# A planned attention-and-MLP kernel: the planner's prices for ScalarE's exponentials and for PE's mode changes, and the issue order that follows from them

## The chip, the cores and the metric

The kernel runs on one core of a Trainium2 chip. A core has a matrix engine (PE, here with its weight loads shown apart as PEld), ScalarE (ACT), VectorE (DVE), GpSimd (POOL) and SyncE (SP), which issues most of the transfers. The engines run side by side, each through its own list of instructions in the order in which the program gives them, and wait for each other on semaphores. The metric is the device time of one execution in microseconds (us), as the median of several runs; before the change it was 745.36 us over 3 runs (745.0 to 745.64). A profile of one execution shows every instruction with its start and its duration. Its span is the time from the first instruction's start to the last one's end.

## The reference

Two branches see the same x (2048 tokens of 512 values, bfloat16) and are mixed by a gate. Branch A is attention with 32 heads of 16 values. Branch B is a normalised MLP with a shift between tokens, and then a second MLP with 1792 hidden values.

```python
x = A_x
g = sigmoid((x * gate_w).sum(-1, keepdims=True))
# A: 32 heads of 16
scores = einsum("bhqd,bhkd->bhqk", q, k) * 16 ** -0.5
o = einsum("bhqk,bhkd->bhqd", softmax(scores), v)
a = o.reshape(B, S, D) @ wo
# B: h = gelu(layernorm(x) @ w1), its quarters shifted by 1, -1, 2, -2 tokens
x1 = x + hs @ w2
b = x1 + gelu(layernorm(x1) @ w3) @ w4
out = g * a + (1 - g) * b
```

## The kernel before

*Tiles.* Attention is cut into 32 rounds: four chunks of 512 queries (c), four groups of eight heads (G), and the even or the odd heads of a group (p). A round has four heads (i = 0 to 3, each on 32 of PE's rows) by 16 blocks of 128 keys (kt): 64 tiles of 128 keys by 512 queries, 2048 in all. For each tile PE multiplies k by q into one of the eight PSUM banks (line 1372). Then the exponential is taken, and PE multiplies the result by V into the round's accumulator (line 1596).

*Two ways to an exponential.* `issue_act` gives two tiles at once (or three) to ScalarE, as one instruction (line 1467); each of its tiles goes through V once. `issue_dve` gives one tile to VectorE, which writes a first approximation of the exponential as the bits of a bfloat16 number (line 1498, called p1). `close_pair` then makes three shifted copies for two such tiles together, on VectorE (line 1541) or on GpSimd (line 1543). All four versions go through V and are summed there, so such a tile costs four multiplications by V. Which tiles go which way is not fixed: it comes out of the planner.

*The planner.* When the program is built, `Sim` plays all engines against each other with a price for each job and writes down the order in which they started; that order is each engine's list of instructions. A job's `hold` is the time after which its engine takes the next job, `lat` what passes from there until others may read the result. `try_engine` starts an engine's best job, sets `t_free` and tells when the job's banks come free: for ScalarE 100 ns behind its hold (`EARLY`), and for a matmul that writes into the bank 195 ns behind it (`USABLE`). `pe_run` plays PE. The four 32-row or 32-column quarters of the array work side by side, 216 ns for a matmul of 512 columns, and a change between q·k (mode "row") and the rest (mode "col") costs `SWITCH`. `pe_pick` decides what PE does next: q·k for ScalarE when banks are free, then q·k for VectorE, and otherwise multiplications by V (`do_pv`) and matmuls of the projections and the MLPs (`do_gen`), as many passes as fit into the time until the next exponential ends (`tr`). An exponential's hold is one line:

```python
hold = 0.833 * 512 * w + 51.5
```

*Knobs.* Some 40 numbers steer these choices. They start from `BASE`, and `STEPS` changes some of them at each of 256 stages of 8 tiles. Those that are spoken of here: `DVE_ALONE` (q·k for VectorE alone may be issued when VectorE comes free in less than so many ns), `DVE_WAIT` (how many tiles may stand waiting for p1), `GP2` (the share of pairs with two of the three shifts on GpSimd; otherwise one), `CAP3` (banks that ScalarE may hold so that three tiles are given at once; 0 means never).

*Around it.* The accumulator of a round goes out through VectorE (line 1617), a division with four small transfers, and a product on GpSimd (line 1635). The rest of ScalarE's list is a few copies at the start, five Gelus over the MLPs' hidden values (line 1214) with their table loads, and two outputs at the end (line 1992).

Of the kernel before, what the change touches and what calls it, by code (L numbers as in the profile page):

```python
# [98 lines left out]
class Job:  # L99
    __slots__ = ("eng", "hold", "lat", "deps", "prio", "fn", "acq", "frees", "at", "done", "start", "seq", "ready", "name", "port", "watch", "deps_tiles", "size", "need", "know")  # L100

    def __init__(self, eng, hold, lat, deps, fn, prio=5, acq=(), frees=(), at=0, name="", port=False):
        self.port = port
        self.eng, self.hold, self.lat, self.deps, self.fn = eng, hold, lat, list(deps), fn
        self.prio, self.acq, self.frees, self.at = prio, list(acq), list(frees), at
        self.done = self.start = None
        self.seq = 0
        self.ready = None
        self.name = name
        self.watch = []  # L110
        self.size = 0
        self.need = None
        self.know = 0

# [75 lines left out]
class Sim:  # L190
    SWITCH = {"row": 104.0, "col": 104.0, "full": 96.0}
    ISSUE = 4.0
    EARLY = {"ACT": 100.0, "DVE": 75.0}
    USABLE = {"ACT": 195.0, "DVE": 168.0}

    def __init__(self, slots):
# [5 lines left out]
        self.t_free = {e: 0.0 for e in ("ACT", "DVE", "POOL", "SP", "PE")}  # L202
        self.t = 0.0
# [126 lines left out]
    def try_engine(self, e):  # L330
# [33 lines left out]
        self.t_free[e] = self.t + j.hold  # L364
        if j.port:
            self.lock = self.t + j.hold
            if e == "DVE":
                self.dve_lock = self.t + j.hold + j.lat
        self.busy[e] += j.hold
        self.log.append((e, self.t, j.hold, j.name))  # L370
        self.push(self.t + j.hold, None)
        soon = [b for b in j.frees if isinstance(b, Call) or b.cls == "bank"] if e in self.EARLY else []
        if soon:
            for b in soon:
                if isinstance(b, Buf):
                    self.bank_know[b.slot] = max(self.bank_know[b.slot], j.know)
                    self.usable[b.slot] = max(self.usable[b.slot], self.t + j.hold + self.USABLE[e])
# [3 lines left out]
        end = self.t + j.hold + j.lat  # L381
# [71 lines left out]
def kernel(  # L453
# [80 lines left out]
        3: dict(SL0=0, B_LOW=3, DVE_WAIT=3, AHEAD=16, MAXU=9, ACC2=0),  # L534
        4: dict(P1_PRIO=0.136),
        5: dict(E_PRIO=0.1),
        6: dict(MAXU=3),
        7: dict(GP2=1, B_LOW=5),
        8: dict(E_PRIO=0.25, JOIN=1),
        9: dict(GP2=0.655),  # L540
        10: dict(GP2=1),
        11: dict(DVE_ALONE=-158),
        12: dict(LIMD=4),
        13: dict(AFIRST=0),
        14: dict(AFIRST=1),
        16: dict(DVE_STOP_L=16, PV_IDLE=0.117, PRESS=26),
        17: dict(IDLE_NS=864, B_LOW=8, ROT=0),
        18: dict(S_PRIO=0.38),
        19: dict(GP3=0.9),
        21: dict(GP3=0.8),  # L550
        22: dict(URG_L=18, PRESS=18),
        24: dict(GP3=0.9, URG_L=12, PRESS=26),
        25: dict(GP3=0.8, DVE_STOP=13, URG_L=18, PRESS=18),
        26: dict(AHEAD2=24, DUE_SH=32, GATE=3),
        27: dict(ROT=1),
        28: dict(SL0=-75, LIMA=2),
        29: dict(MAXG=2),
        30: dict(GP3=0.9, DUE_SH=-9),
        31: dict(GP3=0.8, DUE_SH=32),
        32: dict(GP3=0.967),  # L560
        33: dict(GP3=0.9, DUE_SH=-9),
        34: dict(PV_FULL=0.86, DUE_SH=16),
        35: dict(DVE_ALONE=2, ROT=0),
        36: dict(IDLE_NS=537, ROT=2, GATE=2),
        37: dict(P1_PRIO=0.55, ROWM=3),
        38: dict(SL1=-75, PV_FULL=0.813),
        39: dict(GP3=1, MAXG=1),
        40: dict(ROT=1),
        41: dict(S_PRIO=0.625, SL0=0, B_LOW=3, HOLE=2),
        42: dict(P1_PRIO=0.743, S_PRIO=0.3, GP3=0.8, DVE_STOP=4, DVE_STOP_L=14, URG=8, URG_L=12, DVE_ALONE=362, SL0=-75,  # L570
            IDLE_NS=374, AHEAD=12, PV_FULL=0.97, PV_IDLE=0.731, HOLE=3, MAXG=2, E_PRIO=2, AFIRST=2, ROWM=99, LIMA=4,
            JOIN=0),
        43: dict(ROT=2, AGE=6000),
        44: dict(MAXU=2, AGE=3000),
        45: dict(DVE_STOP_L=16, CAP2=5),
        46: dict(DVE_STOP_L=14, MAXU=3, CAP2=6, AGE=6000),
        47: dict(DVE_STOP=13, IDLE_NS=459, LIMA=3),
        48: dict(E_PRIO=0.4),
        49: dict(AT_SH=118),
        50: dict(ROT=3, ACC2=1),  # L580
        51: dict(GP3=1),
        52: dict(DVE_ALONE=-158, GATE=3, AGE=3000),
        53: dict(PV_FULL=0.813),
        54: dict(P1_PRIO=0.312, AHEAD=24),
        55: dict(BRES=2, MAXG=1),
        56: dict(URG=3, URG_L=18, SL1=-150, ROT=0),
        57: dict(URG_L=12, SL1=60, AGE=20000),
        58: dict(ROT=1),
        59: dict(SL1=130, B_LOW=2, PV_FULL=0.947),
        61: dict(LIMA=2),  # L590
# [24 lines left out]
        88: dict(AHEAD=9),
        89: dict(MAXU=9),
        90: dict(AGE=6000),
        91: dict(LIMA=2),
        93: dict(ROT=2),
        94: dict(ROT=0),  # L620
        95: dict(URG=2),
        96: dict(MAXU=2, JOIN=1),
        97: dict(MAXU=9, JOIN=0),
        98: dict(P1_PRIO=0.55, DVE_WAIT=4, PV_FULL=0.86),
        99: dict(LIMA=4),
        100: dict(URG=8, AT_SH=118),
        101: dict(P1_PRIO=0.414, AT_SH=0, ACC2=0),
        102: dict(AFIRST=1),
        103: dict(P1_PRIO=0.55, B_LOW=0, AHEAD=16, AT_SH=118, AFIRST=2, ACC2=1),
        104: dict(B_LOW=8, AHEAD=9),  # L630
        105: dict(E_PRIO=0.4),
        106: dict(JOIN=1),
        109: dict(CAP2=4),
        110: dict(GP3=0.9),
        111: dict(DVE_ALONE=362, SL1=60),
        112: dict(E_PRIO=2),
        113: dict(DVE_ALONE=500, SL1=-75, PRESS=11),
        114: dict(PV_IDLE=0.117, LIMD=3),
        115: dict(GP3=0.967, DUE_SH=-6),
        116: dict(LIMA=2),  # L640
        117: dict(GP3=0.9, DUE_SH=32, AFIRST=0),
        118: dict(GP3=0.8, B_LOW=5),
        119: dict(URG_L=18, IDLE_NS=700),
        120: dict(DVE_ALONE=2, SL0=-75, BRES=4, AGE=12000),
        121: dict(MAXU=7, ROWM=7, ACC2=0),
        123: dict(GP2=0, DUE_SH=16),
        124: dict(GP2=0.315),
        125: dict(GP2=1, DUE_SH=32, ROWM=5),
        126: dict(GP2=0.5),
        127: dict(DUE_SH=-9),  # L650
        128: dict(GP3=0.9, DVE_STOP_L=12, AT_SH=34),
        129: dict(GP3=0.8, DVE_STOP_L=14, AT_SH=118),
        130: dict(S_PRIO=0.214, GP2=1, GP3=0.9, URG=11, DVE_ALONE=-158, EARLY=64, SL0=0, SL1=0, IDLE_NS=374, BRES=0,
            DVE_WAIT=3, AHEAD=16, PV_FULL=0.97, PV_IDLE=0.5, PRESS=18, MAXU=3, CAP2=6, LIMD=4, GATE=3, ACC2=1, LIMA=3,
            JOIN=0),
# [1370 lines left out]
```

## Time and profile before

| what | value |
|---|---|
| median of 3 runs | 745.36 us |
| span of the profiled execution | 742.9 us |
| TensorE's granted clock | 1.00 in all stretches |
| transfers | 34.60 MB, 47 GB/s on the mean |

The page gives no time of the profiled execution apart from its span. The 2.5 us between span and median are taken as the time that lies around the span.

A line of a group reads: line of the kernel, engine, operation, tile written and tiles read, shape, number; behind the first bar the busy time in us and the mean duration of one in ns; behind the second the time in us that the engine stood idle just before them, and whose end finished the idle time. Busy time counts overlapping instructions once, so it can be far below number times duration. A line of the timeline reads: start and length of a stretch in us, engine, line, operation, number.

### The profile page before, as it was taken

How to read it: one execution, taken by the hardware profiler on the slowest of the kernel's cores; microseconds unless marked ns; L12 is line 12 of the kernel's file. 1: busy time of each engine (PE TensorE's matmuls, PEld its weight loads, DVE VectorE, ACT ScalarE, POOL GpSimd, SP SyncE). 2: the span in 40 equal slices, each digit the busy share in tenths (PEclk: the TensorE clock that was granted, in tenths of full speed). 3: DMA queues.
4: the chain of work that ended last, by engine and by line, in shares of the span. 5: the costliest groups of instructions: out<-in, count | busy, mean ns of one | idle time of the engine just before them, and what ended most of it. 6: DMA issues, size and time to landing. Idle time of an engine off the chain costs nothing.

```text
span 742.9 us, 23801 instructions
## 1 busy us (share of the span) xinstructions
PE 732.1 (99%) x9550; PEld 212.8 (29%) x9550; DVE 678.8 (91%) x1407; ACT 729.8 (98%) x767; POOL 479.0 (64%) x478
## 2 busy tenths in 40 slices
PE   9999999999999999999999999999999999999997
PEld 5443232232222222222322222222222232222222
DVE  5899999999999999898998988999999997999995
ACT  7999999999999999999999999999999999999996
POOL 2247657788776757678557776667777767564441
PEclk9999999999999999999999999999999999999999
DMA  9520234022102132124100110002100000011001
GB/s 199 157 58 5 67 85 91 20 48 67 56 20 63 42 78 55 50 80 95 31 18 14 30 46 15 26 22 48 24 24 18 22 20 20 21 28 24 22 11 43
DMA packets 67094, 34.60 MB, mean 47 GB/s; under 512 B 46748, under 2 KB 62380, under 8 KB 66984
## 3 DMA queue, kind: packets, MB, share of 16 engines
q1 hardware_dynamic: 66040, 32.56, 17.6%
q8 instruction: 74, 1.21, 0.7%
q10 hardware_dynamic: 944, 0.52, 0.2%
q14 instruction: 36, 0.29, 0.1%
HBM read 17.40 MB, written 6.81 MB: 33 GB/s over the span
## 4 chain that ended last, share of the span: by engine, by line
PE 82%; ACT 13%; DVE 3%; issue 2%; ACTq 0%; DVEq 0%
PE banks L1596 29%; PE banks L1372 28%; PE banks L1002 24%; ACT prob L1467 10%; ACT hB L1214 2%; DVE prob L1541 1%; DVE prob L1498 1%; PE banks L981 0%; PE banks L1033 0%; ACT L1214 0%; ACT hT L1214 0%; ACT L1216 0%; PE banks L1127 0%; DVE accsb L1973 0%; DVE accsb L1976 0%
## 5 line engine op out<-in xcount | busy, mean ns | idle before, releaser
L1467 ACT ACTIVATE prob<-banks 128x1024 bf16<-128x1024 f32 (+1 forms) x744 | 685.3, 1146 | 1.1 <-PE banks L1002 0.8
L1543 POOL TENSOR_SCALAR prob<-prob 128x1024 uint16<-128x1024 uint16 x416 | 426.9, 1048 | 218.8 <-DVE prob L1541 97.0
L1498 DVE TENSOR_SCALAR prob<-banks 128x512 uint16<-128x512 f32 x553 | 367.1, 684 | 37.1 <-PE banks L1372 31.9
L1596 PE MATMUL banks<-prob,V 128*17 128x512 bf16 (+1 forms) x3713 | 313.5, 381 | 0.3
L1372 PE MATMUL banks<-q,kT 32*128 32x512 bf16 x2048 | 277.8, 384 | 3.6 <-ACT prob L1467 1.6
L1541 DVE TENSOR_SCALAR prob<-prob 128x1024 uint16<-128x1024 uint16 x418 | 158.4, 431 | 2.9 <-PE banks L1596 0.9
L1372 PEld LDWEIGHTS <-kT 32*128 32x128 bf16 x2048 | 69.9, 91 | 305.6 <-ACT prob L1467 282.0
L1596 PEld LDWEIGHTS <-V 128*17 128x17 bf16 (+1 forms) x3713 | 70.3, 88 | 116.3 <-issue 97.1
L1002 PE MATMUL banks<-xnT,w 128*32 128x512 bf16 x1152 | 96.5, 383 | 0.0
L1002 PE MATMUL banks<-w,hT 128*32 128x512 bf16 x692 | 59.7, 383 | 0.0
L1002 PEld LDWEIGHTS <-w 128*32 128x32 bf16 x1936 | 42.6, 95 | 50.3 <-issue 29.3
L1635 POOL TENSOR_TENSOR oT<-accsb,bcs 128x512 bf16<-128x512 f32 x31 | 39.5, 1275 | 26.1 <-DVE prob L1541 15.8
L1002 PE MATMUL banks<-w,w 128*32 128x256 bf16 (+1 forms) x784 | 41.0, 308 | 0.5 <-DVE prob L1498 0.4
L1002 PE MATMUL banks<-w,hB 128*32 128x512 bf16 x448 | 36.2, 382 | 0.4 <-ACT hB L1214 0.4
L1013 PE MATMUL banks<-wo,oD 32*128 32x512 bf16 x64 | 24.2, 384 | 0.0
L1617 DVE COPY accsb<-banks 128x512 f32<-128x512 f32 x31 | 21.2, 683 | 1.9 <-PE banks L1596 1.4
L1174 DVE BATCH_NORM_STATS2 st<-x_sb 128x6 f32<-128x512 bf16 x32 | 21.4, 678 | 0.0
L1002 PEld LDWEIGHTS <-hT 128*32 128x32 bf16 x692 | 14.7, 95 | 20.5 <-issue 14.2
L1268 DVE CAST hB<-banks 128x512 bf16<-128x512 f32 x28 | 18.9, 682 | 1.0 <-PE banks L1002 0.9
L1268 DVE CAST hT<-banks 128x512 bf16<-128x512 f32 x28 | 19.1, 682 | 0.7 <-PE banks L1002 0.5
L1002 PE MATMUL banks<-wo,oD 128*32 128x512 bf16 x176 | 19.5, 383 | 0.0
L1214 ACT ACTIVATE hT<-hT 128x7168 bf16<-128x7168 bf16 (+1 forms) x3 | 19.4, 6454 | 0.0
(94 smaller groups left out, 258.9 us busy)
## 6 DMA issues: line engine op xcount, KB each, us to landing
bcs<-rr SPq DMA_DIRECT2D x124, 64.0 KB, 2.0
xn_dram<-xn SPq DMA_DIRECT2D x32, 128.0 KB, 1.9
w<-in_B_w_dram SPq DMA_DIRECT2D x5, 512.0 KB
oD<-oT SPq DMA_DIRECT2D x124, 16.0 KB, 1.8
w<-in_B_w_dram SPq DMA_DIRECT2D x4, 448.0 KB
out_dram<-ot SPq DMA_DIRECT2D x14, 128.0 KB, 1.7
x_sb<-in_A_x_dram SPq DMA_DIRECT2D x3, 512.0 KB
w<-in_A_wqkv_dram SPq DMA_DIRECT2D x2, 256.0 KB
```

What stands on the lines that cost most here:

```text
L1002: units.append([Op("col", j, lambda j=j, lf=lf, rf=rf, n0=n0, n1=n1, st=st, sp=sp: nc.tensor.matmul(get()[32 * j:32 * j + 32, n0:n1], lhsT ...
L1013: o = Op("row", i, lambda: nc.tensor.matmul(get(), lhsT=lf(0, P)[rows], rhs=rf()[rows], start=False, stop=True, tile_position=(32 * i, 0), ...
L1174: a = dve(600, deps, lambda: nc.vector.bn_stats(out=sb.slot[:], in_=x_sb[:, t, :]), prio=6, at=at, acq=[sb])
L1214: g = nc.scalar.activation(out=ap, in_=ap, func=ACT.Gelu_apprx_tanh)
L1268: pre.append(evac(g, PSUM_NS, lambda ps, m=m: nc.vector.tensor_copy(out=h2()[:, m, :], in_=ps[:])))
L1372: o = Op("row", i, lambda: nc.tensor.matmul(dst(), lhsT=kT[G][32 * i:32 * i + 32, kt * P:(kt + 1) * P], rhs=qbuf[G, c].slot[32 * i:32 * i ...
L1467: job = act(hold, ops, lambda: nc.scalar.activation(out=prob[:, pb.cut(), :].bitcast(BF16), in_=unit()[:, rb.cut(), :], func=ACT.Exp, scal ...
L1498: return nc.vector.tensor_scalar(out=prob[:, b0.cut() if w == 2 else b0.bufs[h0].slot, :], in0=unit()[:, rb.cut() if w == 2 else rb.bufs[0 ...
L1541: return nc.vector.tensor_scalar(out=cut(k), in0=cut(0), scalar1=float(SHIFT * k), scalar2=None, op0=ALU.add)
L1543: return nc.gpsimd.tensor_scalar(out=cut(k), in0=cut(0 if both else 2), scalar1=1.0, scalar2=float(SHIFT * (k if both else 1)), op0=ALU.mu ...
L1596: return nc.tensor.matmul(one(accs[r])[32 * i:32 * i + n, :], lhsT=lhs(n), rhs=rhs(), start=st and not edge, stop=True, tile_position=(0, ...
L1635: n = gp(1250, d3, lambda: nc.gpsimd.tensor_tensor(out=ob.slot[:], in0=ab.slot[:], in1=bb.slot[:], op=ALU.mult), acq=[ob], frees=[ab, bb], ...
```

## The change

The planner gets another model of ScalarE's exponentials and other prices for PE's changes of mode; with these a new set of `STEPS` is written in. What a job is and what it computes stay as they are.

```diff
 class Sim:
-    SWITCH = {"row": 104.0, "col": 104.0, "full": 96.0}
+    SWITCH = {"row": 95.0, "col": 96.0, "full": 96.0}
     ISSUE = 4.0
+    EXP = SimpleNamespace(step=63.5, begin=50.5, least=171.0, back=369.0, bank=56.0, early=39.0, prob=54.0)
     EARLY = {"ACT": 100.0, "DVE": 75.0}
     USABLE = {"ACT": 195.0, "DVE": 168.0}
...
-        self.t_free[e] = self.t + j.hold
...
+        if j.cols:
+            px, x = j.cols / 1.2, self.EXP
+            last = max(self.act_end + px + x.step, self.t + px + x.least)
+            self.act_end = last
+            self.t_free[e] = max(self.t + px + x.begin, last - x.back)
+            usable, early, end = last + x.bank, last - x.early, last + x.prob
+            self.busy[e] += px + x.step
+        else:
+            self.t_free[e] = self.t + j.hold
...
+            if e == "ACT":
+                self.act_end = self.t + j.hold + 60.0
+            if e in self.EARLY:
+                usable, early = self.t + j.hold + self.USABLE[e], self.t + j.hold + self.EARLY[e]
+            end = self.t + j.hold + j.lat
+        j.over = end
...
-            self.push(self.t + j.hold + self.EARLY[e], lambda: self.release(soon))
+            self.push(early, lambda: self.release(soon))
...
     STEPS = {
-        0: dict(S_PRIO=0.3, DVE_STOP_L=7, SL0=0, IDLE_NS=374, AHEAD=16, AT_SH=69, AFIRST=1, AGE=20000),
-        1: dict(SL0=45, B_LOW=5, DVE_WAIT=1, AHEAD=9),
-        2: dict(AHEAD=7, MAXU=4, ACC2=1),
...
+        0: dict(S_PRIO=0.3, GP2=1, DVE_STOP_L=7, SL0=0, IDLE_NS=864, BRES=2, AHEAD=16, AT_SH=69, HOLE=3, CAP3=5,
+            AFIRST=1, AGE=20000),
+        1: dict(DVE_STOP=2, URG=3, GATE=3, E_PRIO=0.1),
+        2: dict(MAXU=4),
...
+        job.cols = 512 * w
...
-        tr = min((j.start + j.hold + j.lat for j in exps if j.start is not None and j.done is None), default=None)
+        tr = min((j.over for j in exps if j.start is not None and j.done is None), default=None)
```

An exponential of two tiles (1024 columns, `px` = 853.3 ns) now ends 916.8 ns after the one before it, or 1024.3 ns after its own start, whichever is later. ScalarE may take the next job 369 ns before that end, its banks are told free 39 ns before it and may be written 56 ns after it, and its result may be read 54 ns after it. `tr`, the time until which PE's other passes must fit, goes by this end too. `STEPS` has 678 entries before and 1726 after. The knobs named above, as means over the 256 stages:

| knob | before | after |
|---|---|---|
| `DVE_ALONE` (ns) | -37 | 88 |
| `DVE_WAIT` | 3.13 | 3.20 |
| `GP2` | 0.82 | 0.61 |
| stages with `CAP3` of 3 or more | 8 | 35 |

More of the change, by code (lines that the diff above doesn't have):

```diff
@@ L99 @@
 class Job:
-    __slots__ = ("eng", "hold", "lat", "deps", "prio", "fn", "acq", "frees", "at", "done", "start", "seq", "ready", "name", "port", "watch", "deps_tiles", "size", "need", "know")
+    __slots__ = ("eng", "hold", "lat", "deps", "prio", "fn", "acq", "frees", "at", "done", "start", "seq", "ready", "name", "port", "watch", "deps_tiles", "size", "need", "know", "cols", "over")
     def __init__(self, eng, hold, lat, deps, fn, prio=5, acq=(), frees=(), at=0, name="", port=False):
@@ L113, in __init__ @@
         self.know = 0
+        self.cols = 0
+        self.over = None
 class Op:
@@ L376, in try_engine @@
                     self.bank_know[b.slot] = max(self.bank_know[b.slot], j.know)
[L377 removed]
+                    self.usable[b.slot] = max(self.usable[b.slot], usable)
             j.frees = [b for b in j.frees if b not in soon]
[L379 removed]
+            self.push(early, lambda: self.release(soon))
         self.pending -= 1
[L381 removed]
         if e == "SP" and j.hold > 1.5:
@@ L542 @@
[L542 to L554, printed above, removed]
@@ L642 @@
[L642 to L655, printed above, removed]
@@ new lines @@
+        8: dict(P1_PRIO=0.136, GP2=1, DVE_STOP=6, URG=2, DVE_ALONE=-81, SL0=0, B_LOW=5, AHEAD2=16, PRESS=18, MAXU=7,
+            ROT=2, GATE=2, E_PRIO=0.25, AFIRST=1, ROWM=99, LIMA=3, JOIN=1),
+        9: dict(AGE=12000),
+        10: dict(SL0=45),
+        11: dict(GP2=0.655, DVE_STOP_L=12, URG_L=18, DVE_ALONE=2, EARLY=64, SL0=0, BRES=4, AHEAD2=24, MAXU=3, ROT=1,
+            AT_SH=0, AGE=20000),
+        12: dict(PRESS=22, MAXU=5, CAP2=4),
+        13: dict(P1_PRIO=0.279, GP2=0.8, DVE_WAIT=4, ROWM=3),
@@ new lines @@
+        15: dict(P1_PRIO=0.743, S_PRIO=0.178, GP2=0.655, GP3=0.9, DVE_STOP=8, DVE_STOP_L=16, URG=3, URG_L=12, SL0=-150,
+            B_LOW=0, BRES=0, DVE_WAIT=1, AHEAD=3, PRESS=18, MAXU=3, ROT=0, CAP2=6, LIMD=4, ROWM=99),
+        16: dict(SL1=-75, AHEAD=7, MAXU=7),
+        17: dict(P1_PRIO=0.136, DVE_STOP=6, DVE_STOP_L=12, URG=2, DVE_ALONE=-158, SL0=0, SL1=60, IDLE_NS=864,
+            DVE_WAIT=3, AHEAD=16, MAXU=3, ROT=1, HOLE=2),
+        18: dict(DVE_STOP=8, E_PRIO=0.1),
+        19: dict(SL0=130, AHEAD2=32, AFIRST=0),
@@ new lines @@
+        37: dict(MAXG=3, AFIRST=0, LIMA=2, JOIN=1),
+        38: dict(BRES=4, PRESS=22, AFIRST=1),
+        39: dict(P1_PRIO=0.55, GP2=0.655, GP3=1, URG=5, SL1=-75, IDLE_NS=700, B_LOW=5, BRES=0, DVE_WAIT=2,
+            PV_FULL=0.947, PRESS=18, MAXG=1, E_PRIO=0.25, AGE=20000, ROWM=3, LIMA=3),
+        40: dict(GP2=1, GP3=0.967, DVE_STOP=8, URG=8, URG_L=12, DVE_ALONE=138, IDLE_NS=537, B_LOW=8, DVE_WAIT=3,
+            AHEAD=12, PV_FULL=0.813, PV_IDLE=0.25, AT_SH=118, HOLE=0, AFIRST=2, LIMA=2, JOIN=0),
@@ new lines @@
+        70: dict(AGE=3000, ROWM=5),
+        71: dict(P1_PRIO=0.414, DVE_STOP=6, URG=8, DVE_ALONE=-158, SL0=45, SL1=45, IDLE_NS=700, DVE_WAIT=3,
+            PV_FULL=0.947, PV_IDLE=0.25, MAXU=2, ROT=1, DUE_SH=16, HOLE=7, GATE=2, E_PRIO=0.4, AGE=20000, ROWM=99,
+            ACC2=1, LIMA=2),
+        73: dict(ACC2=2),
+        74: dict(EARLY=64, B_LOW=1, E_PRIO=2),
+        75: dict(P1_PRIO=0.1, URG_L=18),
+        76: dict(CAP2=6, ACC2=0),
+        77: dict(AGE=12000),
+        78: dict(GP3=0.633, AHEAD2=32, HOLE=3),
@@ new lines @@
+        79: dict(SL1=0, JOIN=1),
+        80: dict(GP3=1, ACC2=1),
+        81: dict(SL0=0),
+        82: dict(P1_PRIO=0.279, GP3=0.967, DVE_STOP=8, URG_L=12, EARLY=99, B_LOW=8, DVE_WAIT=2, AHEAD=24, AHEAD2=24,
+            PV_IDLE=0.117, MAXU=3, DUE_SH=32, CAP2=4, AGE=20000, ROWM=3, LIMA=4, JOIN=0),
+        83: dict(DVE_WAIT=4, CAP2=6),
+        84: dict(DUE_SH=-14),
+        85: dict(PRESS=15),
+        86: dict(S_PRIO=0.625, GP2=0.15, GATE=3),
+        87: dict(P1_PRIO=0.136, S_PRIO=0.38, GP2=1, GP3=1, DVE_ALONE=-81, IDLE_NS=537, AHEAD=3, PV_IDLE=0.5, PRESS=26,
+            ROT=0, DUE_SH=-9, AT_SH=0, HOLE=7, GATE=2, AGE=6000, ROWM=99, ACC2=2, LIMA=3),
@@ new lines @@
+        95: dict(S_PRIO=0.625, GP3=1, DVE_ALONE=2, EARLY=64, SL1=0, BRES=4, DVE_WAIT=3, AHEAD2=32, PV_IDLE=0.25,
+            PRESS=18, ROT=0, DUE_SH=32, AGE=3000),
+        96: dict(DVE_STOP_L=12, URG=2, AHEAD=12, MAXG=3, AFIRST=0, AGE=9000, JOIN=2),
+        97: dict(SL0=60, DVE_WAIT=1),
+        98: dict(P1_PRIO=0.55, S_PRIO=0.38, GP2=0.655, DVE_STOP_L=7, DVE_ALONE=-158, EARLY=99, BRES=0, DVE_WAIT=4,
+            AHEAD=9, AHEAD2=24, PV_FULL=0.86, PV_IDLE=0.5, MAXU=3, MAXG=1, AFIRST=2, AGE=6000, JOIN=0),
@@ new lines @@
+        99: dict(DVE_STOP_L=14, AT_SH=0, E_PRIO=0.4),
+        100: dict(S_PRIO=0.5, AGE=12000, LIMA=4),
+        101: dict(P1_PRIO=0.2, GP3=0.5, JOIN=2),
+        102: dict(P1_PRIO=0.55, S_PRIO=0.178, GP2=0.15, GP3=1, DVE_STOP_L=12, URG=8, SL0=0, PV_FULL=0.813, MAXU=9,
+            AT_SH=34, MAXG=2, E_PRIO=2, AGE=6000, JOIN=0),
+        103: dict(URG_L=18, DVE_ALONE=500, ACC2=0),
+        104: dict(S_PRIO=0.3, URG_L=12, SL0=-150, SL1=-150),
+        105: dict(SL0=-75, DVE_WAIT=2, AHEAD2=16),
+        106: dict(PRESS=15, LIMA=2),
@@ new lines @@
+        119: dict(GP2=0.3, GP3=0.8, URG=2, DVE_ALONE=362, IDLE_NS=700, B_LOW=5, DVE_WAIT=2, AHEAD=9, AHEAD2=24,
+            PRESS=11, ROT=0, AGE=20000, LIMA=2),
+        120: dict(GP2=1, DVE_ALONE=2, DVE_WAIT=4, AHEAD2=13, PV_FULL=0.947, PRESS=26, CAP2=6, CAP3=4, ROWM=3, ACC2=2),
+        121: dict(HOLE=2, LIMA=3),
+        122: dict(GP2=0.3, SL0=-150, ROWM=5),
+        123: dict(S_PRIO=0.5, GP3=1, DVE_STOP=4, URG=8, URG_L=18, SL0=0, B_LOW=8, AHEAD2=24, PV_FULL=0.86, PRESS=11,
+            MAXU=2, AT_SH=69, HOLE=3, CAP2=5, CAP3=0, GATE=4, ROWM=7, ACC2=1, LIMA=2),
@@ new lines @@
+        124: dict(GP2=0, URG=2, URG_L=12, MAXU=3, GATE=2, JOIN=2),
+        125: dict(PRESS=18, DUE_SH=-14, AGE=9000, JOIN=1),
+        127: dict(DVE_WAIT=3, E_PRIO=0.25, AFIRST=1, ACC2=2, LIMA=3, JOIN=2),
+        128: dict(DVE_STOP=8, DVE_STOP_L=16, SL0=-75, DVE_WAIT=4, PRESS=15, DUE_SH=16, AFIRST=0, AGE=20000, ACC2=1,
+            LIMA=2, JOIN=1),
+        129: dict(URG_L=18, SL0=0, PV_IDLE=0.25, PRESS=18, CAP3=4),
+        130: dict(DVE_STOP_L=14, AHEAD=16, ACC2=0),
+        131: dict(MAXU=2, CAP2=4),
@@ new lines @@
+        146: dict(SL1=-75, PV_IDLE=0.117, MAXU=2, RES=0, AGE=12000),
+        147: dict(DVE_ALONE=-81, B_LOW=2, JOIN=1),
+        148: dict(S_PRIO=0.38),
+        149: dict(S_PRIO=0.178, DVE_STOP_L=12, DVE_ALONE=500, SL1=130, IDLE_NS=864, B_LOW=8, AHEAD=24, MAXU=3, AGE=6000,
+            JOIN=2),
+        150: dict(CAP2=5, E_PRIO=0.25, ACC2=2),
+        151: dict(DVE_STOP=6, SL1=-75),
+        152: dict(CAP3=4, LIMD=5, E_PRIO=2),
+        153: dict(AHEAD=3, DUE_SH=32),
+        155: dict(S_PRIO=0.3, SL0=60, ROWM=7),
@@ new lines @@
+        156: dict(P1_PRIO=0.414, S_PRIO=0.178, GP3=1, DVE_STOP=2, DVE_STOP_L=7, URG=3, URG_L=12, SL0=0, SL1=130,
+            B_LOW=0, BRES=2, DVE_WAIT=2, AHEAD=24, ROT=1, DUE_SH=-14, AT_SH=0, HOLE=3, MAXG=1, CAP3=0, LIMD=3, ROWM=3,
+            ACC2=0, LIMA=4),
+        157: dict(URG_L=18),
+        158: dict(URG=8, DUE_SH=16),
+        160: dict(LIMD=4),
+        161: dict(S_PRIO=0.38, GP2=0.8, GP3=0.9, DVE_STOP_L=12, URG=11, URG_L=12, DVE_ALONE=362, EARLY=64, SL1=45,
+            IDLE_NS=537, BRES=0, PV_FULL=0.813, PV_IDLE=0.5, PRESS=18, MAXU=7, ROT=3, DUE_SH=-9, AT_SH=118, CAP2=6,
+            LIMD=3, AGE=3000, ROWM=7, ACC2=1, LIMA=2, JOIN=0),
@@ new lines @@
+        162: dict(GP2=0.3, BRES=2, MAXU=9),
+        163: dict(MAXU=7, CAP2=5, CAP3=4, LIMD=4),
+        164: dict(SL0=60, MAXU=2),
+        165: dict(MAXU=5),
+        166: dict(P1_PRIO=0.743, DVE_ALONE=2, SL0=0, DUE_SH=0, AT_SH=69, AFIRST=1, LIMA=3),
+        167: dict(P1_PRIO=0.414, GP2=0.655, DVE_STOP=4, DVE_STOP_L=7, URG=2, DVE_ALONE=362, SL0=45, SL1=-75, BRES=0,
+            AHEAD=7, AHEAD2=13, PV_FULL=0.916, PV_IDLE=0.117, PRESS=22, MAXU=7, DUE_SH=-9, AT_SH=118, CAP2=6, CAP3=0,
+            LIMD=5, E_PRIO=0.4, ACC2=0, LIMA=2, JOIN=2),
@@ new lines @@
+        168: dict(DVE_STOP_L=14),
+        169: dict(SL1=60, B_LOW=2, AHEAD=16, ROWM=99),
+        170: dict(S_PRIO=0.178, SL0=60),
+        171: dict(GP2=0.8, AGE=12000, ACC2=2),
+        172: dict(S_PRIO=0.38, DVE_STOP_L=12, URG=5, DVE_ALONE=2, EARLY=99, SL0=0, SL1=-75, B_LOW=0, DVE_WAIT=4,
+            AHEAD=24, AHEAD2=16, PV_FULL=0.813, PV_IDLE=0.25, PRESS=18, MAXU=3, ROT=1, AT_SH=34, HOLE=7, CAP2=4, LIMD=3,
+            E_PRIO=2, AFIRST=0, AGE=3000, ROWM=7, ACC2=1, JOIN=0),
+        173: dict(GP3=0.633),
@@ new lines @@
+        174: dict(GP3=0.9, DVE_ALONE=-81),
+        175: dict(SL0=60),
+        176: dict(GP3=0.967, DVE_ALONE=138, SL0=0, DVE_WAIT=3, PV_FULL=1, PV_IDLE=0.5, DUE_SH=16, CAP2=6, E_PRIO=0.4,
+            ACC2=0, LIMA=4, JOIN=2),
+        177: dict(GP3=0.9, URG_L=18, PV_FULL=0.813),
+        178: dict(EARLY=64, PV_FULL=0.97, LIMD=4),
+        179: dict(GP2=0, GP3=1, URG=3, URG_L=12, DVE_ALONE=500, PV_FULL=1, PRESS=26, MAXU=7, ROT=2, MAXG=3, CAP2=4,
+            LIMD=5, ACC2=1, LIMA=2),
+        180: dict(GP2=1, DVE_ALONE=2, EARLY=99, SL1=45, AHEAD=9, AHEAD2=32, MAXU=3, ROT=0, MAXG=1, CAP2=6, CAP3=5,
+            ACC2=2, LIMA=4),
```

435 lines of the change are left out of this document (219 added, 216 removed).

## The prediction, made before the changed kernel was run

> **What bounds the kernel now.** I read the page's busy shares first, then its chain of waits, then ScalarE alone, since the change is about ScalarE's exponentials.
>
> ```profile
> span 742.9 us, 23801 instructions
> PE 732.1 (99%) x9550; PEld 212.8 (29%) x9550; DVE 678.8 (91%) x1407; ACT 729.8 (98%) x767; POOL 479.0 (64%) x478
> PE 82%; ACT 13%; DVE 3%; issue 2%; ACTq 0%; DVEq 0%
> ```
>
> Three engines stand above 90%, so shares alone name no culprit, and the chain gives most to PE because it follows the last thing that each instruction waited for. The groups of ScalarE by form (busy time, mean duration in ns, then idle time ahead of the group and who ended it) say more:
>
> ```profile
> L1467 ACT ACTIVATE prob<-banks 128x1024 bf16<-128x1024 f32 x739 | 679.8, 1143 | 1.1 <-PE banks L1002 0.8
> L1214 ACT ACTIVATE hB<-hB 128x7168 bf16<-128x7168 bf16 x2 | 12.4, 6177 | 0.0
> L1467 ACT ACTIVATE prob<-banks 128x1536 bf16<-128x1536 f32 x5 | 8.0, 1593 | 0.0
> ...
> L1214 ACT ACT_TABLE_LOAD x3 | 3.8, 1283 | 0.1
> ...
> L1045 ACT COPY w<-banks 128x512 bf16<-128x512 bf16 x2 | 1.2, 586 | 2.2 <-PE banks L1033 2.2
> L1992 ACT ACTIVATE ot<-banks,omg 128x512 bf16<-128x512 f32 x1 | 0.7, 688 | 3.7 <-PE banks L1989 3.7
> L1467 ACT ACTIVATE prob<-banks x744: 1003/1144/1657, 8.7 to 733.6; 128x1024 bf16<-128x1024 f32 x184, 128x1536 bf16<-128x1536 f32 x2
> 459.45 7.55 ACT L1467 ACTIVATE prob<-banks 128x1024 bf16<-128x1024 f32 x8
> ```
>
> From the first exponential (8.7 us) to the last (733.6) ScalarE stood idle only 1.1 us ahead of any of the 744; the 13.1 us that it lacks to the span lie almost wholly before and after. And the 1143 ns of one are no price: 679.8 / 739 is 0.920 us, because they overlap. The last row shows it directly, eight in a row in 7.55 us with a last one of 1.14, that is (7.55 - 1.14) / 7 = 0.916 from end to end. So the pipe of exponentials is full all the time. Its tiles number 739 x 2 + 5 x 3 = 1493, and together they hold the engine 685.3 us:
>
> ```profile
> L1467 ACT ACTIVATE prob<-banks 128x1024 bf16<-128x1024 f32 (+1 forms) x744 | 685.3, 1146 | 1.1 <-PE banks L1002 0.8
> ```
>
> which is 0.459 us a tile. The span reads 742.9 = 685.3 of exponentials + 44.5 of other ScalarE work (729.8 - 685.3: Gelus, table loads, copies) + 13.1 idle. **No order of the same exponentials can be faster by more than about a microsecond. What the change is worth is the number of tiles that it takes from ScalarE and gives to VectorE, times 0.459 us**, less whatever idle time it puts into the pipe.
>
> **What a moved tile costs elsewhere.** VectorE and GpSimd, by form, and PE's multiplication with V:
>
> ```profile
> L1498 DVE TENSOR_SCALAR prob<-banks 128x512 uint16<-128x512 f32 x551 | 364.6, 682 | 37.1 <-PE banks L1372 31.9 <-issue 0.2 <-PE banks L1596 0.2
> L1541 DVE TENSOR_SCALAR prob<-prob 128x1024 uint16<-128x1024 uint16 x415 | 157.7, 432 | 2.9 <-PE banks L1596 0.9 <-ACT prob L1467 0.6
> L1543 POOL TENSOR_SCALAR prob<-prob 128x1024 uint16<-128x1024 uint16 x416 | 426.9, 1048 | 218.8 <-DVE prob L1541 97.0 <-PE banks L1596 38.2 <-PE banks L1372 24.8
>   PE banks L1372: 31.9, 89
> L1541 DVE TENSOR_SCALAR prob<-prob x418: 283/419/1347, 12.3 to 733.4; 128x1024 uint16<-128x1024 uint16 x139, 128x512 uint16<-128x512 uint16 x1
> 460.10 0.61 PE L1596 MATMUL banks<-prob,V 128*17 128x512 bf16 x8
> ...
> 460.64 0.38 PE L1372 MATMUL banks<-q,kT 32*128 32x512 bf16 x1
> ...
> 460.97 0.40 PE L1002 MATMUL banks<-wo,oD 128*32 128x512 bf16 x4
> 461.19 0.39 PE L1596 MATMUL banks<-prob,V 128*17 128x512 bf16 x4
> 461.56 0.39 PE L1372 MATMUL banks<-q,kT 32*128 32x512 bf16 x3
> 461.88 0.61 PE L1596 MATMUL banks<-prob,V 128*17 128x512 bf16 x8
> ```
>
> VectorE now has 2048 - 1493 = 555 tiles. One tile takes 364.6 / 551 = 0.66 us in L1498 and, with 418 shifts for 555 tiles, 0.75 x 0.38 = 0.29 in L1541: 0.95. GpSimd: 0.75 x 1.03 = 0.77, hidden in the 218.8 us that it idles ahead of L1543. PE: such a tile goes through V four times instead of once; a pass of four side by side takes 0.22 (460.97 to 461.19), so three more quarters of a pass are 0.165.
>
> PE has that room. Its queue of weight loads stopped about 700 times for a q·k group; the three largest rows, 684 of them, are these:
>
> ```profile
>   ACT prob L1467: 283.6, 645
>   issue: 9.4, 25
>   DVE prob L1498: 6.0, 14
> ```
>
> A group takes 0.32 (461.56 to 461.88) with the change of mode behind it; a change back costs 0.10 (460.10 to 460.64, less two passes). Of the 9550 matmuls some run beside a q·k group and some are half as long:
>
> ```profile
> L1013 PE MATMUL banks<-wo,oD 32*128 32x512 bf16 x64 | 24.2, 384 | 0.0
> L1002 PE MATMUL banks<-w,w 128*32 128x256 bf16 x544 | 21.1, 275 | 0.5 <-DVE prob L1498 0.4
> L1013 PE MATMUL banks<-w,hT 32*128 32x512 bf16 x12 | 4.6, 384 | 0.0
> ```
>
> So PE needs 700 x 0.32 + 700 x 0.10 + (9550 - 2048 - 76) / 4 x 0.22, less 15 for the half-length ones: 687 us. Some 56 of the span are passes with empty places, and waits.
>
> **The change part by part.** (1) The price of an exponential of two tiles goes from 0.833 x 1024 + 51.5 = 904.5 ns to 853.3 + 63.5 = 916.8. The trace says 916 and 920: the new one is right, and in the planner's account ScalarE grows dearer by 744 x 12.3 ns = 9.2 us. (2) A change of mode goes from 104 to 95 and 96. The planner reckons 216 + 2.5 behind the last matmul's start, so a q·k group came to 322.5 ns and comes to 314.5; the trace shows 0.32, both within its last digit. For 700 pairs PE grows cheaper by 700 x 17 ns = 11.9 us. These two edits cost nothing on the chip by themselves: they make no instruction. They turn the planner's balance by 21 us away from ScalarE and towards the V multiplications that VectorE's tiles cost. (3) The release of banks comes at the exponential's end less 39 ns instead of 1004 after its start; with the measured median of 1144 that is 1105, so groups are planned about 0.1 us later than before, and nearer to what the chip does. (4) The knobs: 1726 entries in place of 678. I averaged each over the 256 stages. VectorE's tile alone (DVE_ALONE) may now be asked for from 88 ns before VectorE comes free, where it was 37 ns after; both shifts of a pair on GpSimd (GP2) fall from 0.82 to 0.61, which puts more shifts on VectorE; groups of three tiles (CAP3 of 3 or more) are allowed in 35 stages, not 8. The last is worth little: 1343.5 ns for three against 1.5 x 916.8 saves 32 ns, and 5 x 35 / 8 = 22 such exponentials instead of 5 give 0.5 us, from none to that. I count none.
>
> No step adds a kind of instruction, a wait or a transfer: the DMAs hang on rounds and rows, whose number stays, and they move with them on SP. The Gelus and table loads stay too; they are covered as long as VectorE has emptied their banks in time (idle 0.0 and 0.1 ahead of them now).
>
> **How many tiles.** No row shows the new number; it is bounded. Below: an earlier request by 124 ns, at the 89 places where VectorE waited for a q·k group, is 11.0 us; a tile needs 0.95 there, and since the span shrinks by 0.459 for each, 11.0 / 1.41 = 8 tiles. Above: all 37.1 us idle ahead of L1498 / 1.41 = 26. Outer ends: nothing or fewer, if the planner spends its freedom elsewhere, and 64.1 us, all of VectorE's idle time, / 1.41 = 45. PE would allow 56 / (0.459 + 0.165) = 90 and so does not decide. I take 15, a little below the middle of 8 and 26, since the 89 waits are 0.36 us each, shorter than one tile, and must first be shifted together. 15 x 0.459 = 6.9 us. The profiled span is 742.9 and the median 745.36; the 2.5 us between them lie outside the span and stay. So 736.0 of span, **738.5 us**.
>
> The rows give one reason for fewer: the longest shift of L1541 took 1347 ns against a median of 419, 0.93 more, about one GpSimd instruction. The Trainium skill, "SBUF — State Buffer", section "SBUF: two separate sides", says why that can be: VectorE in a two-port mode and GpSimd share one port pair, and the one that starts first blocks the other for its whole instruction. By that rule, with one such collision a pair, a tile would cost VectorE 0.46 more, 37.1 / 1.87 = 20 tiles would be the upper end, and half of them would give 740.8.
>
> **The rivals.** (A) *VectorE is filled almost to the end.* For it: GpSimd's 218.8 us and PE's 56. Against: 27 to 45 tiles need idle time that lies ahead of other work too. With 31, 14.2 us: 731.1.
> (B) *VectorE is fuller than it looks.* Pieces of 0.36 us hold no tile of 0.95, and GpSimd's shifts wait for VectorE's already (97.0 us). 5 tiles, 2.3 us: 743.1.
> (C) *The change doesn't do what it says*: the new prices yield another order with 555 tiles, give or take 3. The full pipe makes that 745.4, whatever else is rearranged. For it: many knobs, DVE_WAIT among them, hardly move on average (3.13 to 3.20).
> (D) *Slower: PE's lead is spent.* The pipe is full only because q·k is early: the shortest exponential took 1003 ns, the median 1144, so the usual one stood ready some 0.14 us behind its predecessor. A planner that takes 11.9 us off PE's account packs more V passes between two groups. Where one then comes later than that lead, ScalarE idles, and behind it wait its next exponentials and the V passes that read them. Take such a gap as VectorE's wait for the same groups, 31.9 / 89 = 0.36 us. From 19 gaps on the 6.9 us are eaten; with one exponential in twenty, 37 gaps, 13.3 us: 745.4 - 6.9 + 13.3 = 751.8. For it: three engines over 90%. Against: the new prices are those of the trace, and at the old ones the pipe had 1.1 us of gaps.
>
> **How the numbers follow.** Forecast (8 to 26 tiles, 741.7 to 733.4) 0.50, A 0.12, B 0.13, C 0.09, D 0.16. About 0.2%, 1.5 us, is what a measurement of this kernel can tell from no change: forecast, A and B are faster (0.75), C the same (0.09), D slower (0.16). The range reaches to C above, 746.0, which leaves out D, and below to 730.5, which leaves out the third of A with over 32 tiles (0.04).
>
> **What would show it.** Fewer exponentials in L1467 (about 736 in place of 744), and some 570 tiles in L1498; the end to end spacing still 0.916; idle time ahead of L1467 still below 2 us; less than 37.1 ahead of L1498; some 45 more matmuls in L1596. The forecast is wrong if L1498 keeps its count, or if L1467 shows more than 7 us of idle time: then D holds, and PE's rows would name the late groups.

## The result, and the profile after

The changed kernel takes 736.24 us (735.64 to 738.17, 4 runs) against 745.5 for the kernel before (4 runs, the three from above among them), 9.3 us less; the ratio is 0.9882 with an interval of 0.9867 to 0.9897. Forecast were 738.5 us, with 730.5 to 746.0 as the range.

The page of the changed kernel, span, busy shares and chain by engine:

```profile
span 736.1 us, 23899 instructions
...
PE 724.5 (98%) x9554; PEld 212.2 (29%) x9554; DVE 699.2 (95%) x1493; ACT 720.2 (98%) x751; POOL 453.6 (62%) x452
...
PE 85%; ACT 10%; DVE 2%; issue 1%; DMA 1%; POOL 0%; SPq 0%; ACTq 0%; DVEq 0%
```

Its exponentials on ScalarE by form (line 1577 now), and the outputs at the end:

```profile
L1577 ACT ACTIVATE prob<-banks 128x1024 bf16<-128x1024 f32 x715 | 659.9, 1092 | 1.3 <-PE banks L1482 0.7 <-DVE prob L1652 0.2 <-ACT prob L1577 0.2
L1577 ACT ACTIVATE prob<-banks 128x1536 bf16<-128x1536 f32 x13 | 19.3, 1486 | 0.3
...
L2103 ACT ACTIVATE ot<-banks,omg 128x512 bf16<-128x512 f32 x1 | 0.7, 688 | 3.9 <-PE banks L2100 3.9
```

Its groups of VectorE (p1 is line 1609, the shifts line 1652):

```profile
L1609 DVE TENSOR_SCALAR prob<-banks 128x512 uint16<-128x512 f32 x575 | 377.8, 682 | 17.5 <-PE banks L1482 12.9 <-POOL prob L1654 0.4 <-issue 0.2
L1652 DVE TENSOR_SCALAR prob<-prob 128x1024 uint16<-128x1024 uint16 x477 | 179.0, 423 | 1.9 <-PE banks L1707 0.6
```

And from the page's groups the sums over all forms:

```profile
L1577 ACT ACTIVATE prob<-banks 128x1024 bf16<-128x1024 f32 (+1 forms) x728 | 675.7, 1099 | 1.6 <-PE banks L1482 0.7
L1654 POOL TENSOR_SCALAR prob<-prob 128x1024 uint16<-128x1024 uint16 x390 | 401.2, 1047 | 234.0 <-DVE prob L1652 111.1
...
L1707 PE MATMUL banks<-prob,V 128*17 128x512 bf16 (+1 forms) x3785 | 321.6, 381 | 0.8 <-DVE prob L1652 0.7
```

The shares have hardly moved, and the chain gives PE still more. What has changed are counts. ScalarE has 715 x 2 + 13 x 3 = 1469 tiles instead of 1493, so **24 tiles went to VectorE** (579 instead of 555: the 575 of the row and two instructions of two tiles), and with them 3785 - 3713 = 72 multiplications by V, three for each tile. The price of a tile stayed: 675.7 / 1469 = 0.460 us. The pipe stayed full, with 1.6 us idle ahead of an exponential in place of 1.1.

The account of the span: exponentials 9.6 us less (685.3 to 675.7), other work on ScalarE the same (720.2 - 675.7 = 44.5), its idle time 2.8 us more (736.1 - 720.2 = 15.9 instead of 13.1, half a microsecond of it ahead of exponentials, the rest at the start and behind the last output). That is 6.8 us less, 742.9 to 736.1. The profiled execution was the slowest of the four (738.17 us; the others' spans are 733.4 to 734.0), so the medians show 9.3.

VectorE's time for it came from where the prediction looked: idle time ahead of p1 fell from 37.1 to 17.5 us, and its waits for a q·k group from 89 to 46 (the row of the kernel before stands in the prediction):

```profile
  PE banks L1482: 12.9, 46
```

### The profile page after: what moved, and what is told of

It reads as the page before. It is cut to its first block, busy times and chain, and to the rows that moved or that the text cites. A ratio compares the mean times of both kernels' runs of the same rounds, so it can differ in the third digit from the quotient of the medians.

```text
span 736.1 us, 23899 instructions
## 1 busy us (share of the span) xinstructions
PE 724.5 (98%) x9554; PEld 212.2 (29%) x9554; DVE 699.2 (95%) x1493; ACT 720.2 (98%) x751; POOL 453.6 (62%) x452
## 4 chain that ended last, share of the span: by engine, by line
PE 85%; ACT 10%; DVE 2%; issue 1%; DMA 1%; POOL 0%; SPq 0%; ACTq 0%; DVEq 0%
PE banks L1707 31%; PE banks L1482 29%; PE banks L1112 24%; ACT prob L1577 5%; ACT hT L1324 2%; ACT hB L1324 2%; DMA xn_dram<-xn 1%; ACT L1324 1%; PE banks L1091 1%; DVE prob L1609 0%; DMA pk<-den 0%; PE banks L1143 0%; DVE prob L1652 0%; ACT L1326 0%; DVE xn L1304 0%
## 5 line engine op out<-in xcount | busy, mean ns | idle before, releaser
L1577 ACT ACTIVATE prob<-banks 128x1024 bf16<-128x1024 f32 (+1 forms) x728 | 675.7, 1099 | 1.6 <-PE banks L1482 0.7
L1654 POOL TENSOR_SCALAR prob<-prob 128x1024 uint16<-128x1024 uint16 x390 | 401.2, 1047 | 234.0 <-DVE prob L1652 111.1
L1609 DVE TENSOR_SCALAR prob<-banks 128x512 uint16<-128x512 f32 x577 | 380.2, 683 | 17.5 <-PE banks L1482 12.9
L1707 PE MATMUL banks<-prob,V 128*17 128x512 bf16 (+1 forms) x3785 | 321.6, 381 | 0.8 <-DVE prob L1652 0.7
L1652 DVE TENSOR_SCALAR prob<-prob 128x1024 uint16<-128x1024 uint16 x480 | 179.5, 422 | 1.9 <-PE banks L1707 0.6
L1112 PE MATMUL banks<-xnT,w 128*32 128x512 bf16 x1152 | 89.4, 383 | 0.0
L1112 PE MATMUL banks<-w,hT 128*32 128x512 bf16 x688 | 64.5, 383 | 0.0
L1112 PEld LDWEIGHTS <-w 128*32 128x32 bf16 x1936 | 40.8, 95 | 49.0 <-issue 27.2
L1112 PEld LDWEIGHTS <-hT 128*32 128x32 bf16 x688 | 15.9, 95 | 20.5 <-issue 15.1
L1112 PE MATMUL banks<-w,wq 128*32 128x512 bf16 x256 | 19.6, 387 | 1.0 <-DVE accsb L1728 1.0
```

The source lines that it names most:

```text
L1112: units.append([Op("col", j, lambda j=j, lf=lf, rf=rf, n0=n0, n1=n1, st=st, sp=sp: nc.tensor.matmul(get()[32 * j:32 * j + 32, n0:n1], lhsT ...
L1577: job = act(hold, ops, lambda: nc.scalar.activation(out=prob[:, pb.cut(), :].bitcast(BF16), in_=unit()[:, rb.cut(), :], func=ACT.Exp, scal ...
L1609: return nc.vector.tensor_scalar(out=prob[:, b0.cut() if w == 2 else b0.bufs[h0].slot, :], in0=unit()[:, rb.cut() if w == 2 else rb.bufs[0 ...
L1652: return nc.vector.tensor_scalar(out=cut(k), in0=cut(0), scalar1=float(SHIFT * k), scalar2=None, op0=ALU.add)
L1654: return nc.gpsimd.tensor_scalar(out=cut(k), in0=cut(0 if both else 2), scalar1=1.0, scalar2=float(SHIFT * (k if both else 1)), op0=ALU.mu ...
L1707: return nc.tensor.matmul(one(accs[r])[32 * i:32 * i + n, :], lhsT=lhs(n), rhs=rhs(), start=st and not edge, stop=True, tile_position=(0, ...
```

## The experiments

**Give the 24 tiles back.** Is it the number of tiles, or did the new order win in other ways? In the changed kernel's own order, 12 pairs of VectorE's tiles are turned into exponentials on ScalarE; their shifts and the three further passes through V are left out.

```diff
 def p1():
+    if pr.get("back"):
+        return nc.scalar.activation(out=prob[:, b0.bufs[h0].slot, :].bitcast(BF16),
+                                    in_=unit()[:, rb.bufs[0].slot, :], func=ACT.Exp, scale=0.25)
     return nc.vector.tensor_scalar(
...
 def sh(k=k):
+    if pr.get("back"):
+        return None
```

> The changed kernel in its own order, but 12 pairs of VectorE's tiles (24 tiles, evenly spread) are given back: each of these tiles gets an exponential of its own on ScalarE at the place of its p1, its shifts and its three further passes through V are left out. Theory (ScalarE's pipe of exponentials sets the end, time = tiles on ScalarE x price): 24 x (426.7 + 63.5 ns) = 11.8 us more, 748.0 us, although PE, VectorE and GpSimd all have less to do. Rival (PE or VectorE sets the end, as the chain of waits with 85% PE suggests): no more than the 736.2 of the changed kernel, down to 732 (72 V multiplications fewer, 72 / 4 x 0.22 = 4.0 us).

Measured: 745.23 us (10 runs), ratio to the kernel before 1.0001 (0.9991 to 1.0011). PE, VectorE and GpSimd have fewer instructions than in the changed kernel, and the whole gain is gone. The busy shares of its page, and its exponentials by form:

```profile
PE 730.7 (98%) x9482; PEld 212.8 (29%) x9482; DVE 684.5 (92%) x1448; ACT 731.1 (98%) x775; POOL 438.8 (59%) x437
...
L1577 ACT ACTIVATE prob<-banks 128x1024 bf16<-128x1024 f32 x715 | 663.8, 1101 | 1.4 <-DVE prob L1660 1.3
L1577 ACT ACTIVATE prob<-banks 128x1536 bf16<-128x1536 f32 x13 | 19.5, 1499 | 0.1
L1610 ACT ACTIVATE prob<-banks 128x512 bf16<-128x512 f32 x24 | 16.3, 679 | 0.0
```

The reader is to see the 24 exponentials of one tile (line 1610) in a pipe that is still full. So the 24 tiles account for the gain: what else the new order does differently comes to less than the interval of this comparison, some 0.8 us either way. (A returned tile has an exponential to itself, expected at 0.490 us, where one of a pair takes 0.459; that is 0.7 us for the 24.) The step is 9.0 us where 11.8 were expected.

> The same with 36 pairs, 72 tiles. Theory: 72 x 0.490 = 35.3 us more than the changed kernel, 771.5 us, three times the step of 24 tiles. Rival: under 736.

Measured: 768.9 us. From 24 to 72 tiles the step is 23.7 / 48 = 0.493 us a tile, the 0.490 that was expected; the first 24 cost only 0.375 each. Why is not shown. If the first tiles had found room in small gaps of the pipe, ScalarE's busy time would have grown by less than the 11.8 us; between the two profiled executions it grew by 10.9 (720.2 to 731.1). So gaps may explain about 0.9 of the missing 2.8 us, and the rest stays open.

**How far off is the next engine?** Each exponential on ScalarE takes 480 of a tile's 512 columns, in the order of the changed kernel and in that of the kernel before. The last 32 queries of each block are left out on ScalarE; their places are filled with a constant once at the start.

```diff
-out=prob[:, pb.cut(), :].bitcast(BF16), in_=unit()[:, rb.cut(), :],
+out=prob[:, pb.cut(), 0:480].bitcast(BF16), in_=unit()[:, rb.cut(), 0:480],
```

> The changed kernel in its own order, but each exponential of ScalarE takes 480 of a tile's 512 columns (the last 32 queries of each block are left out there; they are set to zero once at the start). Each exponential of two tiles is 53 ns shorter, 39.2 us in all. Theory (the pipe alone sets the end, with room behind it): the time falls until the next engine is reached. By the profile VectorE is idle 36.9 us and PE needs about 691 of 736, so 10 to 30 us less: 706 to 726. Rival (the plan has used up PE's and VectorE's room, three engines bind at once): less than 4 us less, 732 to 736.

> The same cut in the kernel before. Its PE needs 687 of 743 and its VectorE is idle 64 us. Theory: it falls by more than the changed kernel does, 15 to 39 us, to 706 to 730, and if the new order has spent PE's room (rival D in a mild form), the two come out at nearly the same time. Rival (PE binds before, too): less than 4 us less, 741 to 745.

Measured: the changed kernel falls by 5.3 us only, to 730.92; the kernel before by 17.2, to 728.13 (from 745.28). The first is below what the theory said and close to its rival; the second fits. The page of the changed kernel with short exponentials:

```profile
span 729.1 us, 23909 instructions
...
PE 720.1 (99%) x9554; PEld 215.2 (30%) x9554; DVE 698.4 (96%) x1493; ACT 701.2 (96%) x751; POOL 454.1 (62%) x453
...
PE 93%; DVE 2%; ACT 2%; issue 1%; DMA 0%; POOL 0%; SPq 0%; ACTq 0%; DVEq 0%; POOLq 0%
...
L1578 ACT ACTIVATE prob<-banks 128x960 bf16<-128x960 f32 (+1 forms) x728 | 656.7, 979 | 15.3 <-PE banks L1483 2.6
```

Now ScalarE stands idle 15.3 us ahead of exponentials instead of 1.6, and the chain is PE almost alone. The waits of PE's weight loads (who waited for whom, us, times) show the change of bound, first in the changed kernel:

```profile
PEld L1482 <- ACT prob L1577: 268.9, 644, 0.8
...
PEld L1482 <- issue: 8.2, 23, 0.4
```

and then with the short exponentials:

```profile
PEld L1483 <- ACT prob L1578: 234.0, 568, 0.6
...
PEld L1483 <- issue: 37.1, 99, 0.4
```

76 more q·k groups start as soon as PE itself is through, without an exponential to wait for; 568 still wait for one, so the pipe has not dropped out altogether. The kernel before, with short exponentials, has busy shares in the same order, and PE has the largest part of its chain:

```profile
PE 715.7 (99%) x9550; PEld 216.6 (30%) x9550; DVE 676.9 (93%) x1407; ACT 702.7 (97%) x767; POOL 478.6 (66%) x479
...
PE 73%; DVE 3%; ACT 1%; issue 1%; POOL 0%; DMA 0%; SPq 0%; DVEq 0%; ACTq 0%; POOLq 0%
```

And although the new order is 9.3 us faster as it stands, with short exponentials it is 2.8 us slower than the old one. That fits the work on PE with which it has bought its shorter pipe: 72 more multiplications by V, at the prediction's 0.22 for four 4.0 us.

**Take the load off PE.** Each multiplication by V but a head's first takes 448 of the 512 queries, so 64 queries of each block get one pass only.

```diff
+            m = 512 if st else 448
-            return nc.tensor.matmul(one(accs[r])[32 * i:32 * i + n, :], lhsT=lhs(n), rhs=rhs(), start=st and not edge,
+            return nc.tensor.matmul(one(accs[r])[32 * i:32 * i + n, 0:m], lhsT=lhs(n), rhs=rhs()[:, 0:m], start=st and not edge,
```

> The changed kernel in its own order; each multiplication by V but a head's first takes 448 of the 512 queries (64 queries of each block are summed over the first pass alone). About 3650 matmuls, 912 passes, are 27 ns shorter: 24 us less work on PE, nothing less on ScalarE. Theory (the pipe of exponentials sets the end, PE is next): the 736.2 us stay but for the pipe's gaps, 733 to 737. Rival (PE sets the end, as the chain's 85% says): 24 us less, 712 to 720.

Measured: 733.71 us, 2.5 less. The mean of these matmuls falls from 381 to 356 ns, for 3785 of them, four side by side, an estimated 24 us of PE's work; the pipe stays where it was. The page of this kernel:

```profile
span 733.2 us, 23899 instructions
...
PE 714.2 (97%) x9554; PEld 212.8 (29%) x9554; DVE 698.8 (95%) x1493; ACT 719.0 (98%) x751; POOL 453.3 (62%) x452
...
PE 54%; ACT 31%; DVE 6%; issue 5%; POOL 1%; DMA 1%; SPq 1%; ACTq 0%; DVEq 0%; POOLq 0%
...
L1577 ACT ACTIVATE prob<-banks 128x1024 bf16<-128x1024 f32 (+1 forms) x728 | 674.4, 1156 | 1.9 <-PE banks L1708 1.4
...
L1708 PE MATMUL banks<-prob,V 128*17 128x448 bf16 (+1 forms) x3785 | 295.7, 356 | 0.8 <-DVE prob L1652 0.6
```

The chain of the changed kernel had said 85% PE. That share isn't what a lighter PE is worth.

> The same cut on PE together with exponentials of 480 columns. With the exponentials cut alone the kernel took 730.9 us. Theory (behind the pipe PE is the next engine, 5.3 us away): with PE lighter too the cut of the exponentials pays, 24 us less at most than 730.9, 707 to 718. Rival (VectorE, 96% busy, is the next engine): no less than 729.

Measured: 722.42 us, 8.5 less than with short exponentials alone. So behind the pipe of the changed kernel stands PE, as expected, but the size was missed: the time stops falling 8.5 us on. The page:

```profile
span 721.0 us, 23909 instructions
...
PE 708.2 (98%) x9554; PEld 221.9 (31%) x9554; DVE 698.3 (97%) x1493; ACT 696.6 (97%) x751; POOL 455.1 (63%) x453
...
PE 79%; DVE 11%; ACT 4%; issue 2%; DMA 1%; POOL 1%; SPq 0%; DVEq 0%; POOLq 0%; ACTq 0%
```

VectorE lacks 22.7 us to the span, the least room it had in any run, and its share of the chain has grown to 11%; but the chain is still PE for the most part. What stops the time there, VectorE or the waits of the three engines for each other, was not tried.

**Prices and STEPS apart.** The change consists of prices and of a list of knobs. The old list with the new prices was not tried on the chip, since the planner comes to a standstill with it. The new list with the old prices gives an order:

> The planner before with its old prices, but with the new STEPS. Its order has 544 tiles on VectorE. Theory (tiles set the time; STEPS only fit the prices they were chosen with): 1504 tiles on ScalarE are 11 more than before, 5 us, so 750 at the least, and more by the gaps of an ill-fitting order, 755 to 790. Rival (STEPS alone bring the gain, the prices nothing): 736 to 740.

Measured: 795.53 us (one run). Then a control, the changed kernel with one number off:

```diff
-    SWITCH = {"row": 95.0, "col": 96.0, "full": 96.0}
+    SWITCH = {"row": 97.0, "col": 96.0, "full": 96.0}
```

> Control: the changed kernel with one price off by 2 ns (97 in place of 95 for a change to q·k), same STEPS. Its order has 544 tiles on VectorE, too. If the pair of prices and STEPS is what counts, it is as bad as the new STEPS with all old prices, 750 to 790. If each price counts for itself, a 2 ns error costs next to nothing, 736 to 738.

Measured: 772.02 us (one run). The exponentials of the two, from their pages, STEPS alone first:

```profile
L1559 ACT ACTIVATE prob<-banks 128x1024 bf16<-128x1024 f32 (+1 forms) x745 | 693.2, 1129 | 43.1 <-PE banks L1688 20.8
```

```profile
L1577 ACT ACTIVATE prob<-banks 128x1024 bf16<-128x1024 f32 (+1 forms) x745 | 693.2, 1096 | 19.8 <-PE banks L1707 12.7
```

Both have 1504 tiles on ScalarE and, what the kernels before and after never show, 43.1 and 19.8 us of idle time ahead of exponentials. ScalarE's account holds for them too: 17.5 us more of exponentials than in the changed kernel and 41.5 or 18.2 us more of idle time ahead of them make 59.0 and 35.7, where the spans (793.7 and 770.2) are 57.6 and 34.1 longer. Two nanoseconds on one price cost 36 us. The likely reason, not tried by itself: every knob of the list was chosen for the exact state in which the planner then stands. So taking the change apart says nothing about what the prices are worth.

**The same search for both sets of prices.** Lists for both sets of prices were then made anew, from nothing, by the same short search, twice with the old prices and twice with the new ones:

> Equal search for both sets of prices: STEPS chosen from nothing, block after block of 32 tiles, 30 random changes of knobs for each of the three best so far, with the old prices. Its order has 488 tiles on VectorE. In the planner's own account its last multiplication by V starts at 763.9 us (725.3 for the kernel before, which took 20 us longer on the chip). Theory (the old prices promise too much by some 20 us): 780 to 790. Rival (the prices are as good as the new ones): account and 15 us, 779 or less.

> The same from another random start: 464 tiles, account 770.0 us. Theory: 786 to 796. Rival: 785 or less.

> The same search with the new prices: 506 tiles, account 769.8 us (721.5 for the changed kernel, which took 15 us longer on the chip). Theory (the new prices keep to the chip better, so more tiles go to VectorE and the account misses by 15 us): 782 to 787, a little before the mean of the two with old prices. Rival (at equal search the prices decide everything): over 10 us faster than those.

> The same from the other random start: 521 tiles, account 771.9 us. Theory: 784 to 790; rival as in the run before.

Measured, one run each; the last column is the measured time less the time at which the planner's account starts its last multiplication by V:

| prices | tiles on VectorE | measured | over the planner's account |
|---|---|---|---|
| old | 488 | 782.56 | 18.7 |
| old | 464 | 788.55 | 18.6 |
| new | 506 | 787.75 | 18.0 |
| new | 521 | 785.20 | 13.3 |

The third lies just above the range that was expected. The new prices give VectorE more tiles, and the account misses by less, clearly in one case. But the times are alike: 785.6 us on the mean with the old prices, 786.5 with the new. A short search, some 40 us behind the kernel before and 50 behind the changed one, does not show that the prices by themselves bring anything. For the two kernels themselves the account says 725.3 and 721.5 us, 3.8 apart where the chip shows 9.3, so with the new prices it misses by 15 us and not by 20. How the 9.3 us divide between better prices and a longer search stays open.

## Why the prediction was right, and where it was not

*The pipe of exponentials bounds the kernel, and only its number of tiles counts.* Right, and shown: 24 tiles given back undo the gain to within 0.1%, and an estimated 24 us off PE change the time by 2.5.

*0.459 us a tile.* Right: 0.460 after the change. 24 tiles make 11.0; the exponentials' busy time fell by 9.6 and the median by 9.3. Most of the missing 1.7 us lies in the pipe, which is a little less dense: 0.4590 us a tile became 0.4600, 1.4 us over 1469 tiles.

*15 tiles.* Too few; 24 came, near the 26 that VectorE's idle time ahead of p1 allowed. The term was sized too small because waits of 0.36 us were taken to be hard to join into a whole tile. The new order does join them: 46 of 89 are left, and of 37.1 us there remain 17.5. Nor did a tile need the 1.41 us of idle time that was reckoned: in the profiled executions all of VectorE's idle time fell by 27.2 us (64.1 to 36.9), 1.13 a tile, and 7.6 of it lay elsewhere than ahead of p1, so that 26 was nearly met is in part chance. Rival B built on the same thought and fell with it. With 24 in place of 15 the sum would have been 734.3 us. That the forecast came within 2.3 us is luck to that extent: nine tiles too few, 4.1 us, stand against 1.9 us that the 24 did not bring.

*PE has 56 us of room and does not decide.* This step failed, without harm to the number. The 56 us were counted as if passes with empty places could take other work. With the pipe shortened, the kernel before comes no lower than 728.1 us, so its order had 17.2 us of room behind the pipe, and 5.3 after the change. That this bound is PE is shown for the changed kernel, where a lighter PE brings 8.5 us more; for the kernel before it is read from busy shares and chain alone. With the two prices, 17.2 / (0.459 + 0.165) = 28 tiles is where it would have met the pipe; by the changed kernel, 24 + 5.3 / 0.624 = 32. Both are estimates. They are less room than VectorE's outer bound of 45, and rival A, 31 tiles and 731.1, lay at this limit.

*PE's lead (rival D).* Its mechanism is visible, its price isn't. The median exponential went from 1144 to 1090 ns, so the usual one stands ready 0.09 us ahead instead of 0.14:

```profile
L1577 ACT ACTIVATE prob<-banks x728: 1005/1090/1569, 9.3 to 725.0; 128x1024 bf16<-128x1024 f32 x177, 128x1536 bf16<-128x1536 f32 x5
```

Idle time ahead of exponentials rose by half a microsecond only. The two ill-fitting orders have such idle time, 43.1 and 19.8 us, but by their rows more of it ended with a multiplication by V (20.8 and 12.7) than with a q·k group (12.2 and 6.1), so the rival's late groups are only part of that picture.

*The new prices turn the planner towards VectorE.* Consistent with the result and with the tile counts of the equal searches (506 and 521 against 488 and 464), but as the cause of the 9.3 us it was only argued. Nor was any knob tried by itself, `DVE_ALONE`, which gave the lower bound of 8 tiles, among them.

*GP2 puts more shifts on VectorE.* Right: GpSimd's shifts fell from 416 to 390, VectorE's rose from 418 to 480 (the 477 of the row and three short ones) for 24 more tiles.

*Three tiles at once, counted at nothing.* 13 such exponentials came instead of 5, not 22; at the prediction's 32 ns each the eight are worth 0.3 us.

*One collision a pair, 740.8.* It did not come: the mean shift took 423 ns after 432. The prediction overlooked that the planner of both kernels keeps these jobs apart. GpSimd's jobs and VectorE's shifts are marked `port`, and `try_engine` starts a job so marked only when no other one runs in its account. In the changed kernel's trace 401 of the 480 shifts had no shift of GpSimd beside them, and the longest of those took 486 ns; of the other 79 the longest took 1044, and half no more than 418.

## What to carry to other kernels

Where an engine works through a list without idle time from first to last, multiply its number of instructions by the spacing of their ends: the time is that product plus the engine's other work and the two ends, and an order is worth the work that it moves away. How much can be moved is found by shortening that engine's instructions in a copy, with the order kept: the time to which it falls is what the rest of the kernel needs in that order, and here it said 17 us where a sum of passes had said 56. Which engine sets that next time is seen only when its instructions are shortened as well. And a list of knobs chosen by search can belong to the exact prices that it was searched with: here, with one price off by 2 ns, it lost more than the change had brought.
